# Block attention and routed experts on one core: the ninth block, the first diagonal, the 512-column job and the third gather moved

## The chip, the cores and the metric

One core of one Trainium2 chip. The metric is the device time of one launch in microseconds; a profile of one execution is read beside it. Engines are named as in the profile: PE (TensorE matmuls), PEld (TensorE weight loads), DVE (VectorE), ACT (ScalarE), POOL (GpSimd), SP (the queue that issues most DMAs).

## What is computed

```python
def _attn_ref(q, k, v):                     # 8 batches, 8 heads, 576 positions, 64 wide, float32
    scores = scale * np.matmul(q, k.transpose(0, 1, 3, 2))
    scores = np.where(block_i >= block_j, scores, -1000000000.0)     # blocks of 64, causal by block
    scores = scores - np.max(scores, axis=-1, keepdims=True)
    attn = np.exp(scores)
    attn = attn / (np.sum(attn, axis=-1, keepdims=True) + 1e-09)
    return np.matmul(attn, v).astype(np.float32)

def _moe_ref(x, w_gate, w_local, w1, w2):   # x: the attention, (8, 576, 512); 8 experts, 1024 wide
    ...
            fresh_e = int(np.argmax(logits[b, s]))
            if s == 0 or local_gate[b, s] < 0.5:
                e = fresh_e
            else:
                e = prev_e if prev_e >= 0 else fresh_e
            prev_e = e
            ...
            h = np.maximum(x[b, s] @ w1[e], 0.0)
            out[b, s] = p[e] * (h @ w2[e])
```

Each position goes to one expert: its own best, or the one of the position before, as a gate says. The expert's output is scaled by the softmax share of that expert.

## The kernel before

**Tiling.** 576 positions are nine blocks of 64. A "pair" is two heads of one batch; there are 32 (`NPR`), four per batch. Head 0 of a pair lies in partitions 0 to 63 and head 1 in 64 to 127, so that most matmuls come in twos, one for each half of the PE array.

**The loop.** `for it in range(-2, NPR)` is a software pipeline over the pairs, written out by hand: the instructions of each engine stand in the order of the Python code (manual schedule), and the framework adds only the waits. In one turn, pair a = it+2 is turned (queries and keys transposed), pair c = it+1 has its maxima and its first scores made, pair e = it gets the rest of its scores and its product with the values, and the result of pair x = it-1 is transposed and stored for the gate and the experts.

**One turn on PE**, in order, with the profile's lines: the middle job of the maxima (L588, L594, L568: scores in bfloat16 whose row maximum is taken by DVE, L599 and L604); scores of e in float32 for segments 3 and 2 (`segment`: products L655, and the subtraction of the row maximum as a matmul of ones with a diagonal matrix, L664, `less`); eight pairs of transposes of queries and keys of pair a (`turns`, L990) into the PSUM tiles g0 and g1; the 512-column job of the maxima of c (`top(c, 0)`, L573); products of segments 0 and 1 of c (L655); `tails`: eight transposes of the result of x (L717), two of the ninth block of pair a (L1047), and two matmuls with the identity that turn the ninth block of the result of x (`turn_x_tail`, L709), which stands in 64 columns; the last job of the maxima, for pair a (L573 with 320 and 192 columns, L568); `less` for segments 0 and 1 of c (L664, eight matmuls); then probabilities times values for e (`av`, L689 and L697). Every fourth turn adds the gate sums (L760). Weights of a 64-row half are shown as 64*128 (rows*columns), those of a 64-column half as 128*64.

**What hangs on it.** The maxima go through POOL (`exchange`, L612 to L614) and become diagonals (`shift`: L618 on POOL for blocks 1 to 6, L618 on DVE for blocks 7 and 8; `first_shift`: L625 on DVE, two instructions of 64x64, for block 0). ACT makes the exponentials (`expo`, L671, scores to `prob`), which give the score tiles ps_s back; three such tiles go round, each used for scores and for maxima. ACT also copies the turned keys and queries out of PSUM (L1026, keys first), casts the keys (L1030; POOL casts the queries, L1031), copies the tails (L1057, L1062) and the transposed result (`keep_halves`, L722: four blocks from g1, five from g0).

**Routing** runs beside it on DVE, in steps that a table `plan` ties to turns and places (`at(it, where, f)`). Turn 30 makes the first table of rows, and POOL gathers the rows of the first tiles (`gather`, L791). SP transposes gathered rows (`turn_rows`, L812), and then come the expert matmuls (`up`, L826; `down`, L841), 36 tiles and up to seven more. `cast_x` and `rows_x` (L522 or L527, L535, L539, L542) write each result as bfloat16 rows to DRAM for the gathers; `weights` issues loads of the expert weights from POOL (L63).

## Time and profile before

| what | value |
|---|---|
| median of 3 runs | 448.6 us (448.45, 448.6 and 452.83) |
| time of the profiled execution | 451.19 us |
| its span, first to last instruction | 449.4 us |
| mean granted TensorE clock | 0.992 |
| PE, PEld busy | 432.5 us (96%), 343.1 us (76%) |
| DVE, ACT, POOL busy | 307.8 us (69%), 264.0 us (59%), 302.8 us (67%) |
| HBM read, written | 67.18 MB, 14.97 MB |

The attention takes the first 300 us or so, the experts the rest. A matmul's end is modelled in such a profile, so that the engine looks busy while it waits a tenth of a microsecond: the start times of consecutive matmuls tell more than busy shares. In the rows of the timeline, "x16" is a run of 16 equal instructions, the first number is the start of the first, the second is from there to the end of the last, and a bracket gives idle time before the row and what ended it.

### The profile page before, as it was taken

The numbers are of one execution on the slowest core, as the hardware profiler recorded it, in microseconds if no ns is written. First come the engines' busy times: TensorE is split into PE (matmuls) and PEld (weight loads), VectorE is DVE, ScalarE is ACT, GpSimd is POOL, SyncE is SP. The second block draws the span as 40 slices with busy tenths as digits, with TensorE's granted clock in tenths as the row PEclk, the third lists the DMA queues.
The fourth block names the chain that finished last, engine by engine and source line by source line (L and its number), as shares of the span: only waits on it lengthen the run. The fifth ranks groups of instructions, "written<-read, shape, count | busy, mean of one in ns | idle before, by whom it ended". The sixth has DMA issues, their size and how long they took to land.

```text
span 449.4 us, 19798 instructions
## 1 busy us (share of the span) xinstructions
PE 432.5 (96%) x7842; PEld 343.1 (76%) x7864; DVE 307.8 (69%) x810; ACT 264.0 (59%) x511; POOL 302.8 (67%) x700
## 2 busy tenths in 40 slices
PE   7899999999999999999999999979999999999993
PEld 5688788888888888888888877867777777777771
DVE  4777666768777878786889898765957873343331
ACT  3756665767567757665766576444554655555552
POOL 4656466657556756787666788672778768888853
PEclk9999999999999999999999999998999999999998
DMA  7999699998999996988789998795656745555542
GB/s 150 196 161 186 134 178 188 190 198 161 181 184 178 175 168 130 185 159 175 159 167 189 167 183 165 137 162 85 132 155 155 153 122 142 158 143 149 140 119 75
DMA packets 169886, 71.17 MB, mean 158 GB/s; under 512 B 151424, under 2 KB 158080, under 8 KB 169792
## 3 DMA queue, kind: packets, MB, share of 16 engines
q1 hardware_dynamic: 154640, 38.05, 42.9%
q0 software_dynamic: 13952, 31.52, 34.8%
q8 instruction: 65, 1.06, 1.0%
q10 hardware_dynamic: 1200, 0.30, 0.3%
q14 instruction: 29, 0.24, 0.2%
HBM read 67.18 MB, written 14.97 MB: 183 GB/s over the span
## 4 chain that ended last, share of the span: by engine, by line
PE 87%; DVE 5%; DMA 4%; issue 1%; POOL 1%; ACT 0%; POOLq 0%; ACTq 0%; DVEq 0%
PE ps_s L655 17%; PE ps_h L826 15%; PE g L697 15%; PE ps_o L841 14%; PE g L689 5%; PE ps_s L664 5%; PE ps_m L573 3%; PE g L990 3%; DVE mx L599 2%; PE g L760 2%; DMA scr<-scr 2%; PE g L709 2%; PE g L717 1%; DMA x_rows<-w_bf 1%; PE ps_m L594 1%
## 5 line engine op out<-in xcount | busy, mean ns | idle before, releaser
L671 ACT ACTIVATE prob<-ps_s 128x640 f32<-128x640 f32 (+2 forms) x128 | 103.6, 836 | 48.7 <-PE ps_s L664 47.6
L599 DVE TENSOR_REDUCE mx<-ps_m 128x2 f32<-128x640 f32 (+2 forms) x96 | 100.3, 1044 | 23.8 <-PE ps_m L568 13.1
L655 PE MATMUL ps_s<-plb 64*128 64x320 f32 (+4 forms) x768 | 104.0, 391 | 1.5 <-DVE mx L602 1.1
L655 PEld LDWEIGHTS ps_s<-plb 64*128 64x128 f32 x768 | 69.1, 187 | 21.6 <-issue 12.5
L697 PE MATMUL g<-vt,prob 128*64 128x65 f32 x2560 | 80.5, 222 | 0.0
L697 PEld LDWEIGHTS g<-vt,prob 128*64 128x64 f32 x2560 | 77.6, 138 | 0.3 <-issue 0.2
L841 PE MATMUL ps_o<-w_bf,hT 128*128 x282 | 67.1, 379 | 1.3 <-issue 0.3
L830 ACT ACTIVATE hT<-ps_h 128x512 bf16<-128x512 f32 x76 | 45.4, 597 | 26.6 <-PE ps_h L826 23.0
L844 ACT ACTIVATE o_sb<-ps_o,share 128x512 f32<-128x512 f32 x37 | 25.4, 688 | 42.3 <-PE ps_o L841 33.1
L841 PEld LDWEIGHTS <-hT 128*128 128x128 bf16 x304 | 28.0, 98 | 27.8 <-issue 0.3
L807 DVE COPY natb<-w_bf 128x4096 bf16 x20 | 24.7, 1234 | 31.3 <-PE ps_h L826 28.6
L826 PEld LDWEIGHTS <-natb 128*128 128x128 bf16 x608 | 36.9, 100 | 6.5 <-DVE ints L275 2.4
L807 DVE COPY plb<-w_bf 128x4096 bf16 x20 | 24.6, 1232 | 22.6 <-PE ps_h L826 20.8
L612 POOL COPY mx<-mx 64x2 f32<-64x2 f32 x64 | 11.7, 182 | 40.9 <-DVE mx L599 39.4
L826 PEld LDWEIGHTS <-plb 128*128 128x128 bf16 x608 | 35.5, 98 | 3.9
L664 PE MATMUL ps_s<-diag,ones 64*128 64x448 bf16 (+1 forms) x372 | 36.4, 274 | 0.6 <-DVE diag L618 0.6
L63 POOL DMA_DIRECT2D w_bf<-in_moe_w_dram x56 | 33.6, 599 | 1.4 <-DMA x_rows<-xb 0.4
L1026 ACT COPY plb<-g 128x512 f32<-128x512 f32 x62 | 33.2, 594 | 0.4 <-PE g L990 0.4
L681 POOL MEMSET prob<- 64x128 f32 x128 | 24.1, 203 | 12.3 <-ACT prob L671 6.9
L826 PE MATMUL ps_h<-scr,natb 128*128 128x128 bf16 x416 | 26.9, 226 | 2.3 <-DMA scr<-scr 2.3
L618 POOL TENSOR_TENSOR diag<-negi,mx 128x384 bf16<-128x384 f32 x31 | 25.7, 827 | 2.6
L573 PE MATMUL ps_m<-kh,qh 64*128 64x320 bf16 (+2 forms) x192 | 25.7, 309 | 0.7 <-DVE qh L874 0.3
(288 smaller groups left out, 788.9 us busy)
## 6 DMA issues: line engine op xcount, KB each, us to landing
w_bf<-in_moe_w_dram POOLq DMA_DIRECT2D x48, 256.0 KB
vt<-in_v_dram SPq DMA_DIRECT2D x64, 128.0 KB
natb<-in_k_dram SPq DMA_DIRECT2D x63, 128.0 KB
natb<-in_q_dram SPq DMA_DIRECT2D x63, 128.0 KB
w_bf<-in_moe_w_dram POOLq DMA_DIRECT2D x8, 512.0 KB
x_rows<-w_bf SPq DMA_DIRECT2D x13, 256.0 KB
natb<-in_k_dram SPq DMA_DIRECT2D x32, 32.0 KB
vt<-in_v_dram SPq DMA_DIRECT2D x32, 32.0 KB
```

Source lines behind the costliest of these rows:

```text
L63: nc.gpsimd.dma_start(out=dst[:, e * WE:(e + 1) * WE].rearrange("p (k f) -> p k f", k=n)[:, r:r + m, :], in_=view[e][:, r:r + m, :])
L573: nc.tensor.matmul(ps[:, h, c:c + w], lhsT=qh[rows(h), 64 * b:64 * b + 128], rhs=kh[rows(h), 0:w], start=True, stop=m is None)
L599: nc.vector.reduce_max(mx[:, 7:12:4] if job == 0 else mx[:, b:b + 2], ps[:, :, 0:w], axis=AX)
L655: nc.tensor.matmul(ps[:, h, c:c + n], lhsT=pls[i][rows(h), S + 128 * j:S + 128 * j + 128], rhs=pls[i][rows(h), a:a + n], start=part == 0, ...
L664: nc.tensor.matmul(ps[:, h, c:c + n], lhsT=ones[rows(h), :], rhs=diag[rows(h), a // 64:(a + n) // 64, :], start=False, stop=part == len(SE ...
L671: nc.scalar.activation(p[:, :, SEG0[s]:SEG0[s] + w], ps[:, :, 0:w], func=AF.Exp, scale=scale_attn)
L697: nc.tensor.matmul(g[rows(e), o + 65 * h:o + 65 * h + 65], lhsT=p[:, h, c:c + 64], rhs=t[:, j, h, :], start=(j == 0), stop=(j == m))
L807: nc.vector.tensor_copy(w, w1_bf[:, bass.ds(off, WE)])
L826: nc.tensor.matmul(ps_h[:, f, :], lhsT=w[:, f0 + ko * F:f0 + ko * F + 2 * P - 1:2], rhs=xb[:, ko * P:(ko + 1) * P], start=(ko == 0), stop= ...
L830: nc.scalar.activation(hT[:, half * 4:half * 4 + 4, :], ps_h, func=AF.Relu)
L841: nc.tensor.matmul(ps_o, lhsT=hT[:, fo, :], rhs=w2_bf[:, bass.ds(woff + fo * Dm, Dm)], start=(fo == 0), stop=(fo == FO - 1))
L1026: nc.scalar.copy(pl[:, w * S:w * S + 512], pw[w])
```

## The change

Seven edits, none of which changes what is computed.

1. `turn_x_tail` (two matmuls) goes from `tails` to behind the eight matmuls of `less`, in turns 1 to 29, and writes g1 in place of g0. Its 64 columns are copied by a new ACT instruction (`keep_x_tail`) behind the values' products of blocks 8, 6 and 7 (`av` 4 and 3); the second exponential of c goes behind that copy; the L722 copy from g0 has four blocks.
2. `first_shift` for pairs from 2 on is made by ACT (two activations, Copy with a scale read from SBUF) behind the cast of the keys, where DVE made it behind the middle job.
3. The 512-column job stands between the fourth and the fifth pair of transposes, with `low_shift` on POOL ahead of it.
4. ACT copies the turned queries ahead of the keys (turns 0 on).
5. Turn 30 issues the third gather ahead of the second load of weights there, which moves to where the gather stood.
6. The rows of the result of pair 30 are written to DRAM in the first step of the experts, behind the transposes of the third tile.
7. That result is cast into its own tile `xb`, where it borrowed `qh`.

```diff
@@ -522,8 +522,7 @@
                 cast(xb_two[:, :, i % 2],
                      xs[i].rearrange("p (m s) d -> p m s d", s=2))
                 return
-            xb = xbs[i] = (qh[:, 0:9 * D].rearrange("p (m d) -> p m d", d=D) if i == NPR - 2 else
-                           o_p.tile([P, 9, D], BF16, tag="xb", name="xb", bufs=1))
+            xb = xbs[i] = o_p.tile([P, 9, D], BF16, tag="xb", name="xb", bufs=1)
             cast(xb, xs[i][:, 0:9, :])
 
         def rows_x(i):
@@ -622,9 +621,12 @@
         def first_shift(i):
 
             for h in range(2):
-                nc.vector.tensor_tensor(
-                    (diag1 if i else diag0)[rows(h), 0, :], negi[rows(0)],
-                    mxs[i][rows(0), 9 + h:10 + h].to_broadcast([64, 64]), op=ALU.mult)
+                d, m = (diag1 if i else diag0)[rows(h), 0, :], mxs[i][rows(0), 9 + h:10 + h]
+                if i > 1:
+                    nc.scalar.activation(d, negi[rows(0)], func=AF.Copy, scale=m)
+                else:
+                    nc.vector.tensor_tensor(d, negi[rows(0)], m.to_broadcast([64, 64]),
+                                            op=ALU.mult)
 
         def low_exchange(i):
             exchange(i, slice(1, 4, 2), slice(2, 5, 2), slice(12, 14))
@@ -632,8 +634,6 @@
         def mid_maxima(i, where):
             top(i, 1, where)
             exchange(i, slice(5, 6), slice(6, 7), slice(12, 13))
-            if i > 1:
-                first_shift(i)
 
         def high_maxima(i, where):
             mx = mxs[i]
@@ -718,8 +718,8 @@
 
         def keep_halves(x, g, z):
             xT = new_xT(x) if z else xTs[x]
-            n = 4 if z else 5
-            nc.scalar.copy(xT.rearrange("p (m t) -> p m t", t=64)[:, z::2, :],
+            n = 5 if z == 0 and x >= NPR - 3 else 4
+            nc.scalar.copy(xT.rearrange("p (m t) -> p m t", t=64)[:, z:z + 2 * n - 1:2, :],
                            g[:, 0:64 * n].rearrange("p (m t) -> p m t", t=64))
 
         late = w2_bf[:, E * WE - 2 * S:E * WE].bitcast(F32), scr[:, 544:544 + 2 * S].bitcast(F32)
@@ -963,8 +963,9 @@
         at(30, "start", lambda ps: slots_ps(plan["late"], inva, NTA))
         at(30, "mid", lambda ps: nc.vector.tensor_scalar(toka, inva[:, 0, :], 0.0, 0.0,
                                                          op0=ALU.max, op1=ALU.add))
-        for t in range(XGB):
-            at(30, "turn" if t > 1 else "begin", lambda ps, t=t: gather(t))
+        for t in range(2):
+            at(30, "begin", lambda ps, t=t: gather(t))
+        at(30, "turn", lambda ps: weights(2))
 
         def run(it, where, ps=None):
             for f in plan.get((it, where), []):
@@ -1016,13 +1017,16 @@
                         turned(0, w, pw[w])
                     return
                 for b in range(8):
+                    if b == 4 and it > 0:
+                        low_shift(c)
+                        high_maxima(c, 1)
                     turn_pair(b)
 
             def turned_in():
                 if a == 1:
                     nc.scalar.copy(kh[:, 0:512], pw[1])
                     nc.scalar.copy(qh[:, 0:512], pw[0])
-                for w in (1, 0):
+                for w in (1, 0) if a < 2 else (0, 1):
                     nc.scalar.copy(pl[:, w * S:w * S + 512], pw[w])
 
             def halves_in():
@@ -1046,7 +1050,8 @@
                         for w, (g, c) in enumerate(((g0, 320), (g1, 384))):
                             nc.tensor.transpose(g[:, c:c + 64], tail[rows(w)],
                                                 id_f[rows(w), rows(w)])
-                    turn_x_tail(x, gx[0])
+                    if it >= NPR - 2:
+                        turn_x_tail(x, gx[0])
                 else:
                     g1 = g_tile(1)
                     if on_a:
@@ -1126,7 +1131,7 @@
                 if a + 2 < NPR:
                     load_qk(a + 2)
             if on_e:
-                if on_c:
+                if on_c and not (on_a and it > 0):
                     low_shift(c)
                     high_maxima(c, 1)
             run(it, "top")
@@ -1135,6 +1140,8 @@
                 turn_rows(1)
             if on_a:
                 halves_in()
+            if on_c and c > 1:
+                first_shift(c)
             if on_e:
                 corners(e, 2)
             run(it, "begin")
@@ -1158,18 +1165,23 @@
                 weights({0: 0, 28: 2, 29: 2}.get(it, it < 28 and it not in none))
             if on_x:
                 cast_x(x, nc.gpsimd.tensor_copy if it < NPR - 1 else nc.scalar.copy)
-                rows_x(x)
+                if it < NPR - 1:
+                    rows_x(x)
             if it == NPR - 2:
-                weights(2)
+                gather(2)
                 g1 = g_tile(1)
                 xs[e] = x_one
                 av(e, g1, 4)
                 av(e, g1, 3)
+            ends_due = on_x and it < NPR - 2
             if on_c:
                 for z, ps in enumerate((ps0, ps1)):
                     less(c, ps, z, 0)
                     less(c, ps, z, 1)
-                    expo(c, ps, z)
+                    if not (z and ends_due):
+                        expo(c, ps, z)
+            if ends_due:
+                turn_x_tail(x, g1)
             if on_a:
                 low_exchange(a)
             b_done = (x - 1) // HP if on_x and x >= 1 and (x - 1) % HP == HP - 1 else None
@@ -1194,6 +1206,9 @@
                 if it != NPR - 2:
                     av(e, g1, 4)
                     av(e, g1, 3)
+                if ends_due:
+                    keep_x_tail(x, g1)
+                    expo(c, ps1, 1)
                 norm_last(e, g1)
             run(it, "late", g1)
             if it == NPR - 1:
@@ -1336,6 +1351,8 @@
                 up(t + 1)
             if t + 2 < NTM + 2:
                 turn_rows(t + 2)
+            if t == 0:
+                rows_x(x - 1)
             if t == 1:
                 cast_x(x, nc.gpsimd.tensor_copy)
             if t == 3:
```

How the instructions stand, in the turn of pair e = 14. First PE around the 512-column job, before (g_2948 and g_2949 are g0 and g1 with their numbers; natb holds the loaded queries and keys; each row of 128x64 is one transpose):

```order
L990 MATMUL g_2948<-id_f,natb 128x64
L990 MATMUL g_2949<-id_f,natb 128x64
L573 LDWEIGHTS qh
L573 MATMUL ps_m<-kh,qh 128x512
L573 LDWEIGHTS qh
L573 MATMUL ps_m<-kh,qh 128x512
L655 MATMUL ps_s<-plb 128x448 x2
```

and now:

```order
L991 MATMUL g_2958<-id_f,natb 128x64
L991 MATMUL g_2959<-id_f,natb 128x64
L572 LDWEIGHTS qh
L572 MATMUL ps_m<-kh,qh 128x512
L572 LDWEIGHTS qh
L572 MATMUL ps_m<-kh,qh 128x512
L991 MATMUL g_2958<-id_f,natb 128x64
L991 MATMUL g_2959<-id_f,natb 128x64
```

The job, whose lines are 572 now, has four pairs of transposes ahead of it and four behind. Next PE around the ninth block (L709), before, from the tails to the last job:

```order
L1047 MATMUL g_2994<-id_f,natb 128x64
L1047 MATMUL g_2995<-id_f,natb 128x64
L709 MATMUL g_2994<-id_f,x 64x64 x2
L573 LDWEIGHTS qh
L573 MATMUL ps_m<-kh,qh 128x320
```

and now, first the same stretch, then the end of `less` some thirty rows on:

```order
L1051 MATMUL g_3006<-id_f,natb 128x64
L1051 MATMUL g_3007<-id_f,natb 128x64
L572 LDWEIGHTS qh
L572 MATMUL ps_m<-kh,qh 128x320
L572 LDWEIGHTS qh
L572 MATMUL ps_m<-kh,qh 128x320
```

```order
L664 LDWEIGHTS ones
L664 MATMUL ps_s<-diag,ones 128x192
L664 LDWEIGHTS ones
L664 MATMUL ps_s<-diag,ones 128x192
L709 MATMUL g_3007<-id_f,x 64x64 x2
L689 MATMUL g_3007<-vt_152,prob_150 64x65 x10
```

The two matmuls left the stretch between the transposes and the job and now stand between the subtraction and the values' products. Last ACT, before (a turn without routing steps on ACT has these rows alone):

```order
L1026 COPY plb<-g_2949 128x512
L1026 COPY plb<-g_2948 128x512
L1030 CAST kh<-plb 128x512
L1057 COPY plb<-g_2995 128x128
L722 COPY xT<-g_2995 128x4x64
L1062 COPY plb<-g_2994 128x64
L722 COPY xT<-g_2994 128x5x64
L671 ACTIVATE prob_149<-ps_s 128x2x512
L671 ACTIVATE prob_149<-ps_s 128x2x448
```

and now (a turn earlier in the program; L626 is `first_shift`, L739 is `keep_x_tail`):

```order
L1030 COPY plb<-g_1736 128x512
L1030 COPY plb<-g_1737 128x512
L1034 CAST kh<-plb 128x512
L626 ACTIVATE diag<-negi,mx 64x64 x2
L1062 COPY plb<-g_1785 128x128
L722 COPY w_bf<-g_1785 128x4x64
L1067 COPY plb<-g_1784 128x64
L722 COPY w_bf<-g_1784 128x4x64
L671 ACTIVATE prob_149<-ps_s 128x2x512
L739 COPY w_bf<-g_1785 128x64
L671 ACTIVATE prob_149<-ps_s 128x2x448
```

Two activations stand between the cast and the first tail copy, the last L722 is a block shorter, and a copy stands between the two exponentials.

## The prediction

> **What bounds the kernel now.** I read the page's busy shares and chain first, then the timeline of PE in one turn, start time by start time, because the page alone says only that PE is always busy.
>
> ```profile
> PE 432.5 (96%) x7842; PEld 343.1 (76%) x7864; DVE 307.8 (69%) x810; ACT 264.0 (59%) x511; POOL 302.8 (67%) x700
> PE 87%; DVE 5%; DMA 4%; issue 1%; POOL 1%; ACT 0%; POOLq 0%; ACTq 0%; DVEq 0%
> ```
>
> PE carries 87% of the chain, so a change counts by what it does to the gaps between matmul starts. This is PE's timeline in turn 14:
>
> ```profile
> 149.45 0.23 PE L588 MATMUL ps_m<-kh,qh 64*128 64x64 bf16 x4
> ...
> 150.28 0.30 PE L664 MATMUL ps_s<-diag,ones 64*128 64x320 bf16 x2
> 150.42 0.70 PE L655 MATMUL ps_s<-plb 64*128 64x320 f32 x4
> 150.95 0.30 PE L664 MATMUL ps_s<-diag,ones 64*128 64x320 bf16 x2
> 151.09 0.65 PE L990 MATMUL g<-id_f,natb 64*128 64x64 f32 x16
> 151.58 0.38 PE L573 MATMUL ps_m<-kh,qh 64*128 64x512 bf16 x2
> 151.80 1.84 PE L655 MATMUL ps_s<-plb 64*128 64x448 f32 x16
> 153.47 0.41 PE L717 MATMUL g<-id_f,x 64*128 64x64 f32 x8
> 153.72 0.23 PE L1047 MATMUL g<-id_f,natb 64*128 64x64 f32 x2
> 153.88 0.34 PE L709 MATMUL g<-id_f,x 128*64 128x64 f32 x4
> 154.15 0.31 PE L573 MATMUL ps_m<-kh,qh 64*128 64x320 bf16 x2
> ...
> 154.43 0.57 PE L664 MATMUL ps_s<-diag,ones 64*128 64x448 bf16 x8
> 154.94 0.80 PE L689 MATMUL g<-vt,prob 128*64 128x65 f32 x20
> 155.57 2.50 PE L697 MATMUL g<-vt,prob 128*64 128x65 f32 x80
> 158.00 0.23 PE L588 MATMUL ps_m<-kh,qh 64*128 64x64 bf16 x4
> ```
>
> The turn lasts 158.00 - 149.45 = 8.55 us, and nothing in it is a long wait. The pace of small matmuls is even: 16 transposes in 151.58 - 151.09 = 0.49, 0.061 us a pair; L697, 80 in 2.43, again 0.061 a pair. Two places fall out of this pace, and both lie where the shape of the weights changes between 64*128 and 128*64. The pair L1047 takes 153.88 - 153.72 = 0.16, 0.10 more than a pair. The four L709 take 0.27 where two pairs would take 0.12. So a round trip to the other shape costs 0.25 us, in every turn.
>
> **The ninth block moves (the main term).** Today L1047 to L573 is 154.15 - 153.72 = 0.43 us. With L709 gone one pair of transposes is left, 0.06: 0.37 saved. In the new place the shape changes anyhow, from L664 (64*128) to L689 (128*64), and L709 has the shape of L689. That change is paid today in 154.94 - 154.43 = 0.51 and stays. I add L709 at the pace of its new neighbours, L689's 20 in 0.63: four for 0.13 us. Net 0.24 us a turn; at the least 0.37 - 0.27 = 0.10, if L709 keeps its whole present time. In 29 turns (1 to 29) 0.24 is 7.0 us before losses. TensorEngine Tiling (Array Packing) of the Trainium skill, Tiling Modes, says that changing the tiling mode drains TensorE while another tile of the same mode doesn't; these rows agree, and by that rule, too, two drains of the four in this stretch and the next disappear.
>
> **The 512-column job comes earlier.** It writes the score tile that the exponential of segment 3 still reads. Two pieces show what that costs, ACT in the same turn and the chain in turn 30, where exactly this wait is open already:
>
> ```profile
> 150.62 1.44 ACT L671 ACTIVATE prob<-ps_s 128x640 f32<-128x640 f32 x2 [0.79 <-PE ps_s L664]
> 151.96 1.07 ACT L1026 COPY plb<-g 128x512 f32<-128x512 f32 x2
> 152.90 0.64 ACT L1030 CAST kh<-plb 128x512 bf16<-128x512 f32 x1
> 154.01 0.27 ACT L1057 COPY plb<-g 128x128 f32<-128x128 f32 x1 [0.48 <-PE g L1047]
> 154.18 0.38 ACT L722 COPY w_bf<-g 128x256 f32<-128x256 f32 x1
> ```
>
> ```profile
> 287.20 0.71 ACT prob L671
> 287.91 0.04 issue
> 287.95 0.39 PE ps_m L573 x2
> ```
>
> The first exponential ends at 150.62 + 0.71 = 151.33, and PE can go on 0.04 later, at 151.37. Four pairs of transposes are done at 151.09 + 4 x 0.061 = 151.33. So PE waits 0.04, at most 0.13 (the same plus a pair's time and a half, if the release is slower there). Behind the wait stand the other four pairs, the products and, through g0 and g1, ACT's copies. The products then follow transposes directly, where a 512-column stream hid the loading of their first weights: 0 to 0.06 (one pair), I take 0.03. What the earlier job gives, a diagonal from DVE some 0.1 earlier, nobody waits for in such a turn: L664 at 154.43 follows the job at its own pace.
>
> **ACT gets two activations and a copy.** Before L1057 ACT stands idle 0.48 us, waiting for PE. That is the cover. Nearest rows for a 64x64 activation with a scale from SBUF:
>
> ```profile
> L830 ACT ACTIVATE hT<-ps_h 128x512 bf16<-128x512 f32 x76 | 45.4, 597 | 26.6 <-PE ps_h L826 23.0 <-ACT hT L830 3.3 <-PE g L244 0.3
> L844 ACT ACTIVATE o_sb<-ps_o,share 128x512 f32<-128x512 f32 x37 | 25.4, 688 | 42.3 <-PE ps_o L841 33.1 <-issue 2.4 <-DVE share L816 2.2
> L1062 ACT COPY plb<-g 128x64 f32<-128x64 f32 x32 | 7.4, 231 | 0.0
> L387 ACT ACTIVATE w_bf<-w_bf,nth 128x198 bf16<-128x198 bf16 x1 | 0.5, 473 | 1.0 <-DVE w_bf L381 1.0
> ```
>
> A 64-column copy is 231 ns, and a scale read from SBUF adds 688 - 597 = 91: 0.32 each. Below stands 0.23, above 0.47 (L387, three times the columns). Neighbours overlap: L1026's two of 594 ns take 1.07. So the pair takes about 2 x 0.32 - 0.12 = 0.52 and the next starts 0.12 before its end: 0.40 of ACT's order, inside the pause of 0.48, from which the later copies take some 0.05. Margin: 0.03 us. What is late if it goes: L1057, the L722 copy from g1 behind it, and then L709, which now writes g1 and waits for that copy (ends 154.18 + 0.38 = 154.56; L709 comes at about 154.6), and with it all of PE. I take 0.02 for L709's wait.
>
> ScalarE: Activation LUTs of the Trainium skill, Rules for kernel authors, would have a multiplication on VectorE, not ScalarE, and its section on the table load puts an activation with one such operand at 280 ns + 0.833 a column, an estimate of 333 here, which is that of the rows. By the page's price the pair would be 0.01 later each, and the sum the same within 0.5 us.
>
> The copy of the ninth block reads g1 behind the products of `av` 4 and 3 and delays the second exponential of c: PE ends those at about 154.94 + 0.63 + 32 x 0.061/2 = 156.55, so the exponential ends some 0.25 + 0.91 later, 157.7; the next turn's segment 3 wants its tile at 158.3. Half a microsecond is left, and I cost it at nothing. The queries' copy going first frees POOL's cast; PE wants keys and queries at the same matmul (L573 at 154.15; cast of the keys done at 153.54): nothing.
>
> So one turn: 0.24 - 0.04 - 0.03 - 0.02 = 0.15 us saved.
>
> **Turns that don't pay.** In turn 3 the time is set by a DMA write, not by PE:
>
> ```profile
> 43.41 0.96 SPq L539 DMA_DIRECT2D x_rows<-w_bf  x1
> 49.60 0.72 POOL L522 CAST w_bf<-x 128x640 bf16<-128x640 f32 x1 [3.46 <-DMA x_rows<-w_bf]
> ```
>
> SP issues without a pause up to there and beyond, so the write won't land earlier, and what turns 1 to 3 gained is given back: 26 x 0.15 = 3.9 us.
>
> **DVE is relieved** of two instructions of 218 ns a turn (L625, 62 in the run). It pays where routing makes the last diagonal late, turns 25 and 28:
>
> ```profile
> 245.11 0.59 PE L664 MATMUL ps_s<-diag,ones 64*128 64x448 bf16 x8 [0.25 <-DVE diag L618]
> 271.84 0.59 PE L664 MATMUL ps_s<-diag,ones 64*128 64x448 bf16 x8 [0.36 <-DVE diag L618]
> ```
>
> Together 0.61, since 0.44 less on DVE covers both; 0.6 us (0 to 0.9).
>
> **The passage to the experts.**
>
> ```profile
> 293.54 0.75 POOL L63 DMA_DIRECT2D w_bf<-in_moe_w_dram  x1
> 294.77 3.94 SPq L812 DMA_TRANSPOSE scr<-scr  x2
> 295.10 1.07 POOL L791 DMA_INDIRECT scr<-x_rows,toka  x1 [0.28 <-issue]
> 302.53 3.53 PE L826 MATMUL ps_h<-scr,natb 128*128 128x128 bf16 x32 [2.32 <-DMA scr<-scr]
> 300.20:302.50 2.30, 0.01 (x2) 0.00 (x0) 2.06 (x12) 0.00 (x0) 1.70 (x2) 0.99 0.96 185
> 302.50:305.90 3.40, 3.37 (x33) 3.40 (x33) 0.45 (x3) 0.60 (x1) 0.29 (x1) 0.50 0.82 153
> ```
>
> The last two rows are stretches: length, busy time of PE, PEld, DVE, ACT, POOL, then granted clock, DMA share, GB/s. PE waits 2.3 us for the first transposes, and then runs 3.4 us at a granted clock of 0.50, which costs 1.7 more. The weights' load of 512 KB (2.8 us at 185 GB/s) now starts behind the third gather, about 1.4 us later, and the rows of pair 30 leave SP until the transposes are out. Both take traffic away from the transposes, the gather itself adds some. I take 0.3 us; from -0.5 to 1.2, to 2.9 if the shorter pause leaves the clock up.
>
> **Sum.** 3.9 + 0.6 + 0.3 = 4.8 us. The profiled execution has a span of 449.4 and a time of 451.19; the median of the three runs, 448.6, is 2.6 below that time. I take the same 4.8 off all three: span 444.6, median **443.8 us**. The terms' bounds: at best 26 x 0.24 + 0.9 + 1.2 = 8.3 (440.3); at worst 26 x (0.10 - 0.13 - 0.06 - 0.05) - 0.5 = -4.1 (452.7).
>
> **Rivals.**
> - *L709 keeps its price, or the new waits eat it* (0.22). For: every margin on ACT and at the score tile is under 0.1 us. Against: the pace inside L689 is seen 32 times a turn. With 0.10 gained and 0.10 lost, DVE and the passage are left: 0.9, so 447.7.
> - *SP's issuing sets the pace of the first third* (0.10). For: SP has no pause up to turn 9 or so. Against: PE shows no wait on a DMA there but that in turn 3. Then 9 more turns give nothing: 4.8 - 1.4 = 3.4, so 445.2.
> - *ACT becomes the bound; slower* (0.07). The two activations come to 0.47 each, as L387. The pair then overruns the pause by 0.95 - 0.12 - 0.43 = 0.40; L1057, L722 and so L709 and all of PE behind it are late by as much in each turn: 0.15 + 0.02 - 0.40 = -0.23, 26 times -6.0, with 0.9 from the rest 453.7. It decides from an overrun of 0.2 a turn (that is no change), and beyond 0.35 it is slower by 1%. Against: 64 columns are far from 198.
> - *The forecast* has 0.61, with a range of its own of 440.5 to 446.5.
>
> **How the numbers follow.** 1% (4.5 us) is about what a measurement of this kernel tells from no change. The forecast lies 0.3 beyond that bound, so its chance splits, 0.48 to 0.13; the second rival gives a little to the faster side, 0.02, for a clock that stays up. Faster 0.50; within 1%: 0.13 + 0.22 + 0.08 = 0.43; slower 0.07. The range of 440.5 to 448.9 takes the forecast and the first two rivals in and leaves the third and the far ends out, some 0.17.
>
> **What would show it.** In the profile after, the pair ahead of L572 (320 columns) takes 0.06; from the last L664 to L697 it is 0.13 longer than today's 1.14 (154.43 to 155.57); L572 with 512 columns starts 0.28 behind the first transpose; a turn without routing steps lasts 8.40. L626 has 0.32, and ACT still shows a pause before the copy that was L1057. PE no longer waits for L617 (today's L618) in turns 25 and 28. The forecast is wrong if the turn is above 8.5, if L709 shows a wait on ACT above 0.1, or if the passage takes over 3 us of PE's time.

## The result and the profile after

The changed kernel is slower by 0.9%: 455.5 us median of 20 runs (451.2 to 466.5) against 450.3 of 20 runs of the kernel before (the forecast started from 448.6, the median of three of these); the ratio is 1.009, with a 95% interval of 1.0063 to 1.0117. It is formed without five runs of the changed kernel, of 459.6 us and more, that lay in a slower state. Forecast were 443.8 us and a range of 440.5 to 448.9. The profiled execution of the changed kernel has a time of 455.65 and a span of 453.9 (before 451.19 and 449.4).

First the page's busy times and the engines' shares of the chain that ended last:

```profile
PE 431.2 (95%) x7842; PEld 344.1 (76%) x7864; DVE 300.1 (66%) x750; ACT 292.3 (64%) x600; POOL 302.0 (67%) x700
PE 44%; ACT 21%; issue 9%; POOL 9%; DMA 8%; DVE 5%; SPq 1%; POOLq 1%; ACTq 0%; DVEq 0%
```

TensorE had 87% of the chain before and ScalarE nothing. Now ScalarE has 21%: something on it is waited for again and again. Where, PE's timeline shows in the loop's turn 15, the same turn that the prediction shows (it calls it 14; here turns go by `it`, so that the prediction's turn 3 is turn 4 too, while its turns 25 and 28 are the same here):

```profile
153.02 0.23 PE L587 MATMUL ps_m<-kh,qh 64*128 64x64 bf16 x4
...
154.66 0.41 PE L991 MATMUL g<-id_f,natb 64*128 64x64 f32 x8
154.94 0.39 PE L572 MATMUL ps_m<-kh,qh 64*128 64x512 bf16 x2
155.16 0.42 PE L991 MATMUL g<-id_f,natb 64*128 64x64 f32 x8
155.40 1.91 PE L655 MATMUL ps_s<-plb 64*128 64x448 f32 x16
...
157.38 0.24 PE L1051 MATMUL g<-id_f,natb 64*128 64x64 f32 x2
157.44 0.32 PE L572 MATMUL ps_m<-kh,qh 64*128 64x320 bf16 x2
...
157.72 0.67 PE L664 MATMUL ps_s<-diag,ones 64*128 64x448 bf16 x8
158.61 0.34 PE L709 MATMUL g<-id_f,x 128*64 128x64 f32 x4 [0.22 <-ACT w_bf L722]
158.77 0.76 PE L689 MATMUL g<-vt,prob 128*64 128x65 f32 x20
159.36 2.50 PE L697 MATMUL g<-vt,prob 128*64 128x65 f32 x80
161.79 0.23 PE L587 MATMUL ps_m<-kh,qh 64*128 64x64 bf16 x4
```

The turn lasts 161.79 - 153.02 = 8.77 us; before it was 8.55. Up to L664 it is 0.28 faster (157.72 - 153.02 = 4.70, before 4.98), nearly the 0.30 that the prediction had. From L664 to L697 it takes 1.64 instead of 1.14, and 0.13 was expected for L709's new place. L664 needed 0.50 to its successor before, so L709 could start at 158.22; it starts at 158.61, 0.39 late (the row shows 0.22 of it as idle, since a matmul's modelled end covers the rest). It waits for ScalarE's copy L722, in 26 of the 29 turns. ScalarE's timeline in the same turn:

```profile
154.19 1.44 ACT L671 ACTIVATE prob<-ps_s 128x640 f32<-128x640 f32 x2 [0.79 <-PE ps_s L664]
155.65 1.07 ACT L1030 COPY plb<-g 128x512 f32<-128x512 f32 x2
156.75 0.62 ACT L1034 CAST kh<-plb 128x512 bf16<-128x512 f32 x1
157.28 0.71 ACT L626 ACTIVATE diag<-negi,mx 64x64 bf16<-64x64 f32 x2
158.02 0.27 ACT L1062 COPY plb<-g 128x128 f32<-128x128 f32 x1
158.18 0.38 ACT L722 COPY w_bf<-g 128x256 f32<-128x256 f32 x1
```

The pause ahead of L1062 (L1057 before, 0.48) is gone, and three things filled it. The pair L626 holds ScalarE from 157.28 to 158.02, 0.74 us, where 0.40 was forecast. The cast L1034 starts at 156.75, 0.03 behind the copies' end (155.65 + 1.07 = 156.72), where L1030 of before started 0.13 ahead of it: with the queries copied first, the keys that it reads are those of the copy right before it. And the copies start 0.02 behind the exponentials (before: 0.10 ahead of their end), since the second half of the transposes now stands behind the 512-column job. That is 0.74 + 0.16 + 0.12 = 1.02 against a pause of 0.48. The first tail copy starts 158.02 - 154.19 = 3.83 us behind the first exponential, before 154.01 - 150.62 = 3.39: it is 0.44 late and not 0.54, since the pair starts 0.09 ahead of the cast's end, where the pause began at that end.

### The profile page after: what moved, and what is told of

Read it like the earlier page. It is cut to its first block, busy times and chain, and to the rows that moved or that the text cites. A ratio compares the mean times of both kernels' runs of the same rounds, so it can differ in the third digit from the quotient of the medians.

```text
span 453.9 us, 19711 instructions
## 1 busy us (share of the span) xinstructions
PE 431.2 (95%) x7842; PEld 344.1 (76%) x7864; DVE 300.1 (66%) x750; ACT 292.3 (64%) x600; POOL 302.0 (67%) x700
## 4 chain that ended last, share of the span: by engine, by line
PE 44%; ACT 21%; issue 9%; POOL 9%; DMA 8%; DVE 5%; SPq 1%; POOLq 1%; ACTq 0%; DVEq 0%
PE g L697 15%; PE ps_h L826 7%; ACT plb L1030 6%; PE ps_o L841 6%; POOL out_dram L850 5%; ACT prob L671 5%; PE g L689 4%; PE ps_s L655 4%; ACT kh L1034 4%; ACT diag L626 3%; DVE mx L598 3%; DMA out_dram<-o_sb,tok2s 3%; DMA x_rows<-w_bf 2%; PE g L760 2%; PE g L709 2%
## 5 line engine op out<-in xcount | busy, mean ns | idle before, releaser
L671 ACT ACTIVATE prob<-ps_s 128x640 f32<-128x640 f32 (+2 forms) x128 | 108.3, 849 | 35.5 <-PE ps_s L664 34.6
L655 PE MATMUL ps_s<-plb 64*128 64x320 f32 (+4 forms) x768 | 106.7, 398 | 1.1 <-DVE mx L601 0.9
L655 PEld LDWEIGHTS ps_s<-plb 64*128 64x128 f32 x768 | 69.4, 189 | 19.2 <-issue 11.0
L697 PE MATMUL g<-vt,prob 128*64 128x65 f32 x2560 | 80.8, 222 | 0.0
L697 PEld LDWEIGHTS g<-vt,prob 128*64 128x64 f32 x2560 | 77.8, 138 | 0.3 <-issue 0.2
L826 PEld LDWEIGHTS <-natb 128*128 128x128 bf16 x608 | 35.4, 98 | 8.0 <-DVE hl L282 3.5
L807 DVE COPY plb<-w_bf 128x4096 bf16 x20 | 24.6, 1231 | 21.9 <-PE ps_h L826 19.8
L664 PE MATMUL ps_s<-diag,ones 64*128 64x448 bf16 (+1 forms) x372 | 38.9, 274 | 0.0
L826 PEld LDWEIGHTS <-plb 128*128 128x128 bf16 x608 | 35.4, 98 | 4.2 <-issue 0.4
L850 POOL DMA_INDIRECT out_dram<-o_sb,tok2s x17 | 28.6, 1680 | 11.8 <-issue 8.7
L1030 ACT COPY plb<-g 128x512 f32<-128x512 f32 x62 | 33.3, 589 | 1.9 <-PE g L991 1.0
L991 PEld LDWEIGHTS g<-id_f,natb 64*128 64x128 f32 x496 | 25.7, 139 | 8.0 <-issue 4.9
L1075 POOL CAST kh<-plb 128x64 bf16<-128x64 f32 x32 | 7.6, 237 | 35.2 <-ACT plb L1062 29.3
```

Source lines behind the costliest of these rows:

```text
L655: nc.tensor.matmul(ps[:, h, c:c + n], lhsT=pls[i][rows(h), S + 128 * j:S + 128 * j + 128], rhs=pls[i][rows(h), a:a + n], start=part == 0, ...
L664: nc.tensor.matmul(ps[:, h, c:c + n], lhsT=ones[rows(h), :], rhs=diag[rows(h), a // 64:(a + n) // 64, :], start=False, stop=part == len(SE ...
L671: nc.scalar.activation(p[:, :, SEG0[s]:SEG0[s] + w], ps[:, :, 0:w], func=AF.Exp, scale=scale_attn)
L697: nc.tensor.matmul(g[rows(e), o + 65 * h:o + 65 * h + 65], lhsT=p[:, h, c:c + 64], rhs=t[:, j, h, :], start=(j == 0), stop=(j == m))
L807: nc.vector.tensor_copy(w, w1_bf[:, bass.ds(off, WE)])
L826: nc.tensor.matmul(ps_h[:, f, :], lhsT=w[:, f0 + ko * F:f0 + ko * F + 2 * P - 1:2], rhs=xb[:, ko * P:(ko + 1) * P], start=(ko == 0), stop= ...
```

## The experiments

The comparisons are each with the kernel before, run on the same chip. "Plain turn" is the distance of two L587 (L588) starts in a turn without gate sums or routing.

**What fills ScalarE.** Theory A says: ScalarE's order sets L709. The rivals: the job between the turns (B), or the place of the ninth block itself (C). Four kernels undo one part each, or do one alone.

Both activations back on VectorE:

```diff
-                if i > 1:
-                    nc.scalar.activation(d, negi[rows(0)], func=AF.Copy, scale=m)
-                else:
-                    nc.vector.tensor_tensor(d, negi[rows(0)], m.to_broadcast([64, 64]),
-                                            op=ALU.mult)
+                nc.vector.tensor_tensor(d, negi[rows(0)], m.to_broadcast([64, 64]), op=ALU.mult)
...
             exchange(i, slice(5, 6), slice(6, 7), slice(12, 13))
+            if i > 1:
+                first_shift(i)
```

> The changed kernel with the two first_shift instructions back on VectorE, in their old place; all else as changed. Theory A (ScalarE's order): in the changed kernel the pair takes 0.74 us of ScalarE (148.32 to 149.06), not 0.40, because neither activation overlaps its successor; with 0.16 for a cast that now waits on the copy right before it and 0.13 for copies behind the later transposes that overruns the 0.48 pause, and L709 waits for the copy of g1: 0.37 us a turn. Without the pair the copy of g1 ends about 149.25 on the same clock and L709 waits 0.1 at most: turn 8.40 to 8.45 us instead of 8.78, 29 x 0.35 = 10 us off, some 0.6 back in two turns where VectorE is late: 0.988 of the kernel before. Theory B (the 512-column job between the turns delays transposes, copies and with them L709): L709 still waits 0.2 or more, turn 8.65 or above, ratio 1.002 or above. Theory C (the ninth block in its new place costs TensorE itself): turn 8.6 to 8.8, with no wait shown on ScalarE.

Measured: plain turn 8.44, as A said, and no wait at the moved block. In turn 15 L707 (the change's L709) follows the subtraction, L662 here, by 0.55, in the change by 0.89:

```profile
153.93 0.59 PE L662 MATMUL ps_s<-diag,ones 64*128 64x448 bf16 x8
154.48 0.34 PE L707 MATMUL g<-id_f,x 128*64 128x64 f32 x4
154.65 0.76 PE L687 MATMUL g<-vt,prob 128*64 128x65 f32 x20
```

Ratio 0.9998 (0.996 to 1.0035): 0.9% better than the change (measured in another series of runs), but no faster than before; A's 0.988 fell.

The keys first again, the activations on ScalarE:

```diff
-                for w in (1, 0) if a < 2 else (0, 1):
+                for w in (1, 0):
```

> The changed kernel with the keys copied ahead of the queries again; all else as changed. Theory A: the cast of the keys no longer waits on the copy right before it (gap +0.03 becomes -0.13), ScalarE is 0.16 earlier at the pair, L709 too: turn 8.62 instead of 8.78, 29 x 0.16 = 4.6 us off, ratio 0.999; the later cast of the queries may give 0.05 a turn back at L572, then 1.002. Theories B and C: no change, ratio 1.009.

Measured: plain turn 8.62, the cast overlaps its predecessor by 0.11 again; ratio 1.0072 (1.0034 to 1.011). The turn is A's, the time is not: 0.999 to 1.002 was expected. In the trace the 30 turns of the loop take 276.6 us together, where those of the change take 276.2, so what the plain turn gained went into longer turns (more of that below).

The 512-column job behind all transposes again:

```diff
                 for b in range(8):
-                    if b == 4 and it > 0:
-                        low_shift(c)
-                        high_maxima(c, 1)
                     turn_pair(b)
...
-                if on_c and not (on_a and it > 0):
+                if on_c:
```

> The changed kernel with the 512-column job behind all 16 transposes again; all else as changed. Theory A: ScalarE's copies start 0.13 earlier (overlapped with the exponential again) and L709 with them: turn 8.65, ratio 1.000 to 1.003. Theory B: the whole of the wait goes, turn 8.40 to 8.45, ratio 0.988. Theory C: turn 8.75, ratio 1.008.

Measured: plain turn 8.65; ratio 1.0045 (1.0014 to 1.0076). ScalarE's copies overlap the exponential by 0.10 again. So each of the three fillers of ScalarE, taken out alone, shortens the plain turn: the order of the copies by its whole 0.16, the job by 0.13, the pair by 0.34 (by then nothing waits any more). As an account of the turn A stands; B and C, which wanted 8.40 and 8.75 in the last, fall.

The ninth block's move alone, on the kernel before (L709 behind the subtraction, its copy and the second exponential behind `av`):

```diff
-                    turn_x_tail(x, gx[0])
+                    if it >= NPR - 2:
+                        turn_x_tail(x, gx[0])
...
+            if ends_due:
+                turn_x_tail(x, g1)
...
+                if ends_due:
+                    keep_x_tail(x, g1)
+                    expo(c, ps1, 1)
```

> The kernel before with the ninth block moved behind the subtraction and nothing else of the change. Theory A: ScalarE keeps its old order, its copy of g1 is done when L709 comes (wait 0 to 0.05), and the two shape changes saved show whole: turn 8.31 to 8.36 instead of 8.55, 26 turns x 0.19 to 0.24 = 5 to 6 us off, ratio 0.986 to 0.989. Theory C (the move itself is not worth its place): turn 8.5 or above, ratio 0.997 or above.

Measured: plain turn 8.39 (8.45 in some). In turn 15 L709 follows L664 by 0.52, so it waits for nothing; L664 itself now starts 0.07 behind its predecessor's pace, on VectorE's last diagonal, which ends 0.05 before. That is the difference to 8.31. Ratio 1.0021 (0.9985 to 1.0058): 0.16 a turn is saved, and the time doesn't show it. A's 0.986 to 0.989 fell here too; C's ratio (0.997 or above) was met, though its turn (8.5 or above) was not.

**Why the pair takes 0.74.** The kernel before, with four activations of one form in ScalarE's pause in each of five turns (the fifth, turn 23, is as turn 6 with float32 results, and came out as turn 6):

```diff
+                for o, i_, s in {
+                        6: [(dum[lo], negi[lo], mx[lo, 9:10]), (dum[hi], negi[lo], mx[lo, 10:11])],
+                        9: [(dum[lo], negi[lo], mx[lo, 9:10]), (dum[lo], negi[lo], mx[lo, 10:11])],
+                        15: [(dum, negi, mx[:, 9:10]), (dum, negi, mx[:, 10:11])],
+                        17: [(dum[lo], negi[lo], 2.0), (dum[hi], negi[lo], 2.0)],
...
+                }[it] * 2:
+                    nc.scalar.activation(o, i_, func=AF.Copy, scale=s)
```

> The kernel before with four extra activations (unused results) in ScalarE's pause in each of five turns, each turn another form: 6 as in the change (64 partitions, scale from SBUF, the two writing different halves); 9 the same, all to one half; 15 128 partitions, scale from SBUF; 17 64 partitions, constant scale; 23 as in the change with f32 results. If a scale from SBUF keeps an activation from overlapping its successor, the gaps are +0.02 in 6, 9, 15 and 23 and -0.1 in 17; if 64 partitions do it, +0.02 in 17 too and -0.1 in 15; if the two halves do, -0.1 in 9. Each takes 0.34 alone.

ScalarE's timeline in turns 6, 9 and 17:

```profile
72.63 1.47 ACT L1150 ACTIVATE dum<-negi,mx 64x64 bf16<-64x64 f32 x4
74.12 0.27 ACT L1059 COPY plb<-g 128x128 f32<-128x128 f32 x1
...
100.09 1.50 ACT L1150 ACTIVATE dum<-negi,mx 64x64 bf16<-64x64 f32 x4
101.49 0.24 ACT L1059 COPY plb<-g 128x128 f32<-128x128 f32 x1
...
173.63 1.10 ACT L1150 ACTIVATE dum<-negi 64x64 bf16<-64x64 f32 x4
174.75 0.27 ACT L1059 COPY plb<-g 128x128 f32<-128x128 f32 x1
```

Look at where the copy starts against the group's end. In turns 6 and 17, where every second activation reads one half of the partitions and writes the other, it starts 0.02 behind (72.63 + 1.47 = 74.10). In turn 9, where all stay in their half, it starts 0.10 ahead (101.59), and so in turn 15 with 128 partitions (0.09). The scale's source is not it: turn 17 has a constant. Within turns 9 and 15 the four stand 0.03 apart too, but there each writes the very elements that the one before wrote, and carries a wait for it. That isn't what holds up the pair of the change: its two write different halves of one tile, and the trace shows no wait with the second, nor with the second of turns 6 and 17, and yet it stands 0.025 behind the first. So a ScalarE instruction that reads partitions 0 to 63 and writes 64 to 127 overlaps neither its predecessor nor its successor here; the other direction was not run.

Two experiments in the place of the change. First, two activations that stay in their half (unused results, two tiles), with the real pair on VectorE:

```diff
             if on_c and c > 1:
-                first_shift(c)
+                for h in range(2):
+                    nc.scalar.activation(dum[h][rows(0)], negi[rows(0)], func=AF.Copy,
+                                         scale=mxs[c][rows(0), 9 + h:10 + h])
```

> The changed kernel with first_shift back on VectorE and, in its place on ScalarE, two activations of the same size whose unused results go to the half that their input is in. Theory A2 (what costs 0.74 us is that the second activation writes another half than it reads, and ScalarE does not overlap it with either neighbour, as the gaps of the dummies in turns 6 and 17 showed and those in turns 9 and 15 did not): the pair now takes 0.50 of ScalarE's order, L709 waits 0.1 to 0.15, turn 8.54 to 8.58 between 8.44 without a pair and 8.78 with the one of the change. Theory A1 (any two activations cost that): 8.78.

```profile
155.02 0.62 ACT L1033 CAST kh<-plb 128x512 bf16<-128x512 f32 x1
155.54 0.58 ACT L1144 ACTIVATE dum<-negi,mx 64x64 bf16<-64x64 f32 x2
156.03 0.24 ACT L1061 COPY plb<-g 128x128 f32<-128x128 f32 x1
```

The pair now holds ScalarE 156.03 - 155.54 = 0.49 us instead of 0.74, with an overlap of 0.09 on both sides; plain turn 8.50, a little better than 8.54 to 8.58. Second, only the half that stays in its half is left on ScalarE:

```diff
-                if i > 1:
+                if i > 1 and h == 0:
                     nc.scalar.activation(d, negi[rows(0)], func=AF.Copy, scale=m)
...
             exchange(i, slice(5, 6), slice(6, 7), slice(12, 13))
+            if i > 1:
+                first_shift(i, (1,))
```

> The changed kernel with only the first of the two activations left on ScalarE (the half that it reads), the other back on VectorE in its old place. Theory A2: the single one overlaps its neighbours and takes 0.25, the cast's wait 0.16, which the pause covers: L709 waits 0.05 at most, turn 8.43. Theory V (VectorE has work enough in the turns with routing steps that each 0.22 us there costs TensorE time: with both on VectorE those turns gave back 4 us): half of that comes off too: ratio 0.995 to 0.997, where both on VectorE gave 0.9998. Against V: 1.000.

Measured: plain turn 8.44, and no wait at the moved block; ratio 1.0016 (0.9973 to 1.0058), which is what was expected against theory V. Two more: both instructions on GpSimd (the code below), and one activation on ScalarE with the keys first (two of the codes above together):

```diff
-                if i > 1:
-                    nc.scalar.activation(d, negi[rows(0)], func=AF.Copy, scale=m)
+                eng = nc.gpsimd if i > 1 else nc.vector
+                eng.tensor_tensor(d, negi[rows(0)], m.to_broadcast([64, 64]), op=ALU.mult)
```

> The changed kernel with the two instructions on GpSimd, behind the cast of the queries. That cast ends at 148.12 and L664 wants the first diagonal at 148.95, 0.83 later; two 64-column products there are 0.5 to 0.7 by a 64-column cast of 0.24 and the 384-column shift of 0.82. Theory A2 and V: no wait at L709, plain turn 8.43, and routing turns as in the changed kernel since VectorE is relieved of both: 1.009 - 9.9/450 = 0.987. Rival: GpSimd is late itself, L664 waits 0.1 to 0.3 for the diagonal: turn 8.6, ratio 0.995 to 1.000.

> As the kernel with one activation left on ScalarE, and the keys copied ahead of the queries again. Theory A2: ScalarE has 0.16 more room that nobody waits for, plain turn 8.43; GpSimd's cast of the queries ends 0.4 later, just when L572 wants it: no gain, the same ratio to 0.3% more.

Measured: plain turn 8.44 in both; ratios 1.0108 (1.0039 to 1.0176), where 0.987 was expected, and 1.0054 (1.001 to 1.0098). Every one of these has the short turn, and none is faster than the kernel before. So a second question stood open: where does a turn that is 0.11 us shorter than before's go?

**Where the short turns go.** I added up the 30 turns from the first L587 with `it` = 0 to the one of turn 30, in each trace, and beside it the sum of the shortest that each turn was in its group of equal plain turns; the difference is what single long turns cost.

| plain turn | kernels (traces) | shortest turns | sum | in long turns |
|---|---|---|---|---|
| 8.78 | the change; with two buffers | 274.4 | 276.2; 275.9 | 1.8; 1.5 |
| 8.55 | before (two traces); fewer loads; two buffers | 269.0 | 270.7, 272.8; 271.1; 272.2 | 1.7, 3.8; 2.1; 3.2 |
| 8.44 | VectorE; one half; GpSimd; keys first | 265.2 | 270.1; 278.1; 279.9; 273.2 | 4.9; 12.9; 14.7; 7.9 |
| 8.44 | fewer loads; two buffers (three kinds) | 265.2 | 271.0; 276.2, 272.3, 276.4 | 5.8; 11.0, 7.1, 11.1 |

In these traces, one execution each, the kernels with the shortest plain turn lose the most in a few long ones, and the sums stay between 270 and 280. So do those of the traces that the table leaves out: 274.6 and 276.1 for the ninth block's move with one buffer and with two, 276.6 for the keys first, 274.6 for the job behind all transposes, 275.6 for the pair in one half. What a long turn is made of, the timeline of the kernel with one half shows around turn 19:

```profile
181.61 3.93 SPq L506 DMA_DIRECT2D natb<-in_k_dram  x1
...
193.13 1.09 SPq L538 DMA_DIRECT2D x_rows<-w_bf  x1
...
198.67 0.71 POOL L522 CAST w_bf<-x 128x640 bf16<-128x640 f32 x1 [4.38 <-DMA x_rows<-w_bf]
199.41 0.36 DVE L558 TENSOR_TENSOR x<-g,rs 128x192 f32<-128x192 f32 x1 [3.94 <-POOL w_bf L522]
...
199.92 0.24 PE L200 MATMUL g<-id_f,scr 9*1 9x9 f32 x4 [3.51 <-DVE rs L549]
```

Read it downwards: SP needs 3.93 us to issue one load; the write of the rows behind it in SP's queue goes out only at 193.13; GpSimd's cast of the next pair wants that write's buffer and waits 4.38; VectorE waits for the cast, TensorE for VectorE. This is the chain of the prediction's turn 3 (POOL L522, 3.46), in other turns. L522 waits for x_rows 3.5 and 6.0 us in the two traces of the kernel before, 7.8 in that of the change, and 7.1, 15.5, 11.1 and 11.4 in the four with short turns of the third row.

The wait is not all that such a turn costs. From TensorE's restart in this trace on, its granted clock (third number from the end) is 0.50:

```profile
199.92:205.73 5.81, 5.81 (x48) 3.99 (x50) 3.45 (x6) 2.46 (x5) 4.21 (x12) 0.50 0.82 160
```

So turn 19 is 3.5 us above the shortest of its kind and turn 20, which has no wait of that length, 2.7. Five traces have a wait of TensorE of over 3.5 us in the loop: this one, GpSimd (turn 28), and three of the kernels with two buffers (turns 25, 25 and 28). All five have a clock of 0.50 for 2.9 to 5.8 us behind it, and no other trace has it in the loop. With half of that time lost, an estimate, it is 1.5 to 2.9 us of what they lose in long turns. 

Three attempts to cut the late writes follow.

The first: a second trace of the kernel before, and then this kernel and the change with both activations on VectorE, each with 36 of the 64 quarters of weights not loaded (a memset of 0.96 us on GpSimd takes each load's place, so the experts compute with zeros):

```diff
-                    load_weights(quarters[0], m)
+                    (clear_weights if 4 <= it < 24 else load_weights)(quarters[0], m)
```

> The kernel before, unchanged, for a trace from the chip that the next ones run on. All theories: the plain turn 8.55 us; if the trace of another chip differs, it does so in the turns in which the rows' writes are late.

> The kernel before, but in turns 4 to 23 each load of expert weights (256 KB) is replaced by a memset of the same quarter, so the experts' results are not those of the reference. Theory D (the transfers set a second pace: SP issues nearly without a pause and the 16 DMA engines are busy 0.9 to 1.0 of a turn, so rows are written late and POOL's cast L522 waits for a buffer): the stalls of L522 on x_rows go but the plain turn stays 8.55, 1 to 3 us off in all, ratio 0.993 to 0.998. Theory R (what the shorter turns lose is lost in the routing steps themselves, not to transfers): no change, 1.000.

> The changed kernel with first_shift back on VectorE, and in turns 4 to 23 the same memsets in place of weight loads (experts' results again not the reference's). Theory D: every plain turn takes 8.44 and the turns with routing steps lose their stalls on x_rows too; it gains 29 x 0.11 = 3 us on the kernel before with the same memsets: ratio to the kernel before 0.985 to 0.992. Theory R: the losses in turns 9 to 25 stay, ratio 0.998 to 1.001.

Measured: 1.0051 (1.0013 to 1.0089) and 1.0096 (1.0056 to 1.0136). In the traces L522's wait shrinks to the one in turn 4 (3.4 and 4.0), and between turns 5 and 17 only one turn of the short-turn kernel is 0.3 above the shortest. But several of its turns from 18 to 28 stay long, and there TensorE waits for no transfer: for GpSimd's cast of the queries in turn 22 (0.51 us; the memsets on GpSimd may have a part in it) and for VectorE in turns 25 (0.31) and 28 (0.30 and 0.31). In the loop nothing was gained: 271.1 us against 270.7 and 272.8, and 271.0 against 270.1 with all loads. The whole times decide less: behind the last L826 both kernels take 14.4 us to their end, where the other eighteen traces take 9.5 to 11.0, since GpSimd's closing instruction takes 9.1 us in place of 4.2 to 5.7. Without these 3.4 to 4.9 us the ratios would be some 0.994 to 0.998 and 0.999 to 1.002, an estimate from one trace each: theory D's forecast for the first kernel, about theory R's for the second. So D is not shown and not refuted; R holds for the late turns. The second trace of the kernel before has the plain turn of 8.55; where it differs from the first, a late write is one reason only: 0.7 in turn 2 and 0.6 in turn 14 are waits of TensorE that show no releaser.

The second attempt is a second buffer for the rows, so that the cast waits for a write two pairs older:

```diff
-        xb_two = w2_bf[:, E * WE - WE:E * WE - WE + 20 * D].rearrange(
-            "p (m z s d) -> p m z s d", z=2, s=2, d=D)
+        xb_twos = [w2_bf[:, E * WE - WE + 20 * D * n:E * WE - WE + 20 * D * (n + 1)].rearrange(
+            "p (m z s d) -> p m z s d", z=2, s=2, d=D) for n in range(2)]
```

> The changed kernel with one activation left on ScalarE, and two buffers in turn for the rows that GpSimd casts and SP writes. Theory D (the late write holds up the cast, the cast VectorE, VectorE TensorE): L522 no longer waits on x_rows, the turns of 9.3 to 12.4 go, plain turn 8.43: 7 us less than with one buffer, some 3 us less than the kernel before with two: ratio 0.985 to 0.992. Theory V (VectorE's routing steps take it back): within 0.2% of the kernel before with two buffers. Rival E (it goes elsewhere): 1.000.

> The kernel before with the two buffers and nothing else. Theory D: the 1.5 us in the turn that starts at 48.95 go, and those of other executions (6.0 us of waiting in the second trace, of which TensorE paid about 2): ratio 0.994 to 0.998. Theories V and E: 0.998 to 1.001.

> The changed kernel, both activations on ScalarE, with the two buffers. Theory A2 with D: plain turn 8.78 as before, the two or three long turns shortened: 1.009 less 0.004 to 0.007: 1.002 to 1.005. If the buffer were the whole of the loss of the change: 0.990.

> The kernel before with the ninth block moved and the two buffers. Theory D: plain turn 8.39 to 8.45 and no long turns, 26 x 0.12 = 3 us less than the kernel before with the two buffers: ratio 0.987 to 0.991. Theory V: the turns with routing steps, late on VectorE, give it back: 0.995. Rival E: 1.000 as with one buffer.

Measured: 1.0059 (1.0021 to 1.0097), 1.0054 (1.0021 to 1.0087), 1.0162 (1.0127 to 1.0197) and 1.0133 (1.0095 to 1.0171). L522 never waits for x_rows in any of them, and yet none is faster; the kernel before with the two buffers is itself slower by 0.5%, and the first is level with it, as theory V expected. Three are spoiled by my choice of the place: VectorE's scratch in L324 lies in the second buffer and waits 3.8, 2.0 and 4.7 us for transfers in turn 25 of the first, third and fourth (14.8, 10.2 and 14.6 us long). The view names loads there, which share their semaphores with the writes of the rows; that the writes are meant is read from the code. The next two, the third attempt, have the buffer in another place, and the second of them six weight loads later:

```diff
+        xb_twos = [w[:, n:n + 20 * D].rearrange("p (m z s d) -> p m z s d", z=2, s=2, d=D)
+                   for w, n in ((w2_bf, E * WE - WE), (w1_bf, E * WE - 20 * D))]
...
-        none = 3, 16, 22
+        none = 3, 9, 13, 16, 18, 22
```

> The changed kernel with one activation left on ScalarE and the second buffer of the rows in a part of the first weights that is loaded last. Theory D: plain turn 8.44, no wait on x_rows, turn 25 (14.77 with the shared scratch) 9.0: the attention part ends at 283 to 286, where the two traces of the kernel before have 286.0 and 288.5; ratio 0.990 to 0.998. Rival E (stalls of TensorE without a releaser, of 0.3 to 1.1 us each, and the experts' part, which the change doesn't touch, vary by more than is saved): 0.998 to 1.005.

> The same, and the weight loads of turns 9, 13 and 18 (six) come in turns 27 to 29. If the load of the transfers makes the stalls without a releaser, those in the middle turns become fewer and the attention part ends 1 to 2 us earlier than in the other kernel; the transposes and gathers of turn 30 may pay for it: 0.990 to 0.998. If not, the same as the other within 0.2%.

Measured: 1.0102 (1.0041 to 1.0164; single runs from 450.1 to 461.8) and 1.0049 (1.0001 to 1.0098). The attention part of the first ends at 287.8. The view of waits of this kernel tells what took L522's place:

```profile
PE g L691 <- DMA vt<-in_v_dram: 1.7, 4, 0.9
POOL xb L526 <- DMA x_rows<-xb: 1.6, 1, 1.6
```

The columns are us in total, times, the longest. Now TensorE itself waits for the values that SP loads, four times. In the second kernel the loads that came later hold up the rows of pair 28: the cast L526 waits 6.3 us there, TensorE 4.5, and turn 28 takes 17.1. No version beats the kernel before.

## Why the prediction was wrong

**The step that failed** is in the part on ScalarE: "Neighbours overlap: L1026's two of 594 ns take 1.07. So the pair takes about 2 x 0.32 - 0.12 = 0.52 and the next starts 0.12 before its end: 0.40 of ACT's order, inside the pause of 0.48". The duration was about right (0.34 to 0.35 against 0.32). The overlap was not: I took it from two copies that stay in their partitions, and the second activation doesn't. Of the 0.34 by which 0.74 exceeds 0.40, 0.09 is a matter of sizes (0.49 for the pair in one half), 0.25 is the other half. The pause of 0.48 and the 0.10 by which the pair overlaps the cast add up to 0.58, so 0.74 overruns them alone; that is a sum, no run has this filler alone. The page ScalarE: Activation LUTs of the Trainium skill, What ACT_TABLE_LOAD costs, says that activations in a row overlap by about 93 ns; the traces agree where the halves are the same (0.09) and not where they differ (a gap of 0.025).

**Two costs that I set at nothing.** "Margin: 0.03 us" had no room for either. The order of the copies I weighed by GpSimd's cast and TensorE alone; on ScalarE the cast of the keys came to stand behind the copy that it reads: 0.16 (the kernel with the keys first has it back). The job between the transposes I charged to TensorE alone (0.04 + 0.03; from L587 to L655's sixteen it is 2.38 against 2.35 before, so it cost 0.03), but the later transposes delay ScalarE's copies too: 0.12. All three signs of being wrong that the prediction names came: the turn above 8.5 (8.77), L709's wait on ACT above 0.1 (0.22), the passage above 3 us (3.36). A smaller slip: its turn 3 is turn 4, so that 25 turns are left to pay and not 26, 0.15 us of the sum.

**The sign came from the rival with 0.07.** "L1057, L722 and so L709 and all of PE behind it are late by as much in each turn: 0.15 + 0.02 - 0.40 = -0.23": the turn went from 8.55 to 8.77 or 8.78. Its place was met, by another route: not 0.47 an activation, but no overlap and the two costs above. That the size agrees is luck. By the prediction's own bound of 1% the ratio of 1.009 still counts as no change, for which it gave 0.43, though its interval leaves no change out. The chance was too small because I asked only whether an activation of 64 columns can be as slow as one of 198.

**What held.** The ninth block: L1051 to L572 is 0.06 (forecast 0.06), L709 costs 158.77 - 158.61 = 0.16 (0.13), and alone it brings 0.16 a turn, 0.07 less than it would if VectorE's diagonal came in time. VectorE's relief in turns 25 and 28: TensorE waits for no L617 in the changed kernel, and turns 25 and 28 take 8.78 and 10.16 instead of 8.98 and 10.69: 0.7, forecast 0.6, and that with a plain turn that is 0.23 longer. In the short-turn kernels the two instructions matter more: with both on VectorE turns 25 and 28 take 9.06 and 10.75 at the shortest; with both on GpSimd turn 25 takes 8.44, and with one left on ScalarE turn 28 takes 10.07.

**The passage** could not be judged from one trace. The changed kernel waits 3.36 for the transposes (2.32 before), but TensorE's clock then stays at 1.00. That can't be put down to the change: the second trace of the kernel before, in two stretches around its first L826, doesn't have the slow clock either (seventh and later columns as in the prediction's rows):

```profile
302.60:304.40 1.80, 0.07 (x4) 0.01 (x1) 1.63 (x9) 0.00 (x0) 1.14 (x2) 1.00 1.19 237
304.40:306.20 1.80, 1.78 (x32) 1.80 (x33) 0.95 (x6) 0.60 (x1) 0.86 (x1) 1.00 1.53 220
```

From turn 30's start to the 32nd L826 the same kernel took 19.8 us in one execution and 17.7 in the other; the changed kernel took 19.3. A term of 0.3 us can't be seen in that. Two series of runs are steadier: there the five traces with the edits of turn 30 take 17.3 us and the three without 17.9 to 18.0, so they may bring 0.6; no run has these edits (5 to 7) alone.

**The forecast would have failed without ScalarE's cost, too.** With the pair off ScalarE the plain turn is 8.44, 0.11 less than before where 0.15 was forecast, and the time is that of the kernel before. The rival on SP's issuing named a suspect that the traces show at work, at too small a price: it took 1.4 us off, and the short-turn kernels lose 5 to 15 us in long turns where before loses 2 to 4. In part this is shown: the waits for rows, values and keys are late transfers on SP's queue, in the routing turns it is VectorE, and behind the longest waits TensorE's clock adds to the price. What stays open is the common cause. Fewer loads and a second buffer each took the named waits away, and others came, without a gain in the loop; whether SP's queue, the load of all transfers or VectorE keeps these 30 turns at 270 us and more was not separated.

## What to carry to other kernels

Before moving an instruction into an engine's pause, add up the order that it takes there from neighbours of the same form, partitions included, and ask of each instruction in the pause's run-up whether it now reads what its predecessor writes. A pause of 0.48 us with a margin of 0.03 is no cover. And when the longest engine is shortened by 1 to 2% a turn, look for the second pace first: the sum over all turns, long ones apart, tells more than the plain turn. Look there at the granted clock as well, since the waits above 3.5 us cost a third or more on top that way, by the estimate above.

## What the hardware showed that was not expected

- A ScalarE instruction that reads partitions 0 to 63 and writes 64 to 127 stands 0.024 us clear of both neighbours; in its own half it overlaps them by 0.09 to 0.12. That makes two 64-column activations cost 0.74 us (28 of 30 turns in the changed kernel) or 0.49 (25 of 30 with the pair in one half); in the other turns the copy behind them comes later for other reasons.
- The length of a pause alone doesn't tell whether TensorE's clock falls. Ahead of the first L826 it fell to 0.50 for 3.4 us behind waits of 2.3 (before), 2.0 (the kernel before with fewer loads) and 3.6 us (one half with the keys first), and not behind 1.7 (the second trace of before), 2.7 (the last kernel) and 3.4 (the change). In the loop it fell behind all five waits above 3.5 us, and the longest wait behind which it didn't was 2.3.
- In two of the series of runs the experts' part took 136 to 140 us between its 32nd and its last L826, whatever the kernel, with waits of TensorE of 0.3 to 1.1 us; in the others 132.6 to 134.7. The kernel before had medians of 455 to 456 in those and 450 in the others. A trace of one chip is not to be laid beside one of another to half a per cent.
